# First halves of K's and Q's weights ahead of b1 in the transfer queue, their products in alternation, and all queues ordered anew from there

## The chip, the core and the metric

The kernel runs on one core of one Trainium2 chip. The core has a matrix engine (PE, or TensorE; its weight loads are shown apart as PEld), a vector engine (DVE, or VectorE), an activation engine (ACT, or ScalarE), a third elementwise engine (POOL, or GpSimd), and a queue engine (SP, or SyncE) that issues all transfers of this kernel. Each engine works through its own list of instructions in order, and waits at an instruction until the semaphores it needs have reached their counts. The metric is the time of the whole program on the device, in microseconds (us), smaller is better. Of several executions the median is given.

## The reference

Two transformer layers over 2048 rows of 512 columns, each with an attention and an MLP part, both layers with the same weights; all in bfloat16.

```python
def _A_ref(x, wqkv, wo):
    B, S, D = x.shape
    H = 32; Dh = D // H; W = 256
    qkv = (x @ wqkv).reshape(B, S, 3, H, Dh).transpose(2, 0, 3, 1, 4)
    q, k, v = qkv[0], qkv[1], qkv[2]
    scores = jnp.einsum("bhqd,bhkd->bhqk", q, k) * (Dh ** -0.5)
    idx = jnp.arange(S)
    mask = (idx[:, None] - idx[None, :] >= 0) & (idx[:, None] - idx[None, :] < W)
    p = _softmax(jnp.where(mask[None, None], scores, -1e9), axis=-1)
    o = jnp.einsum("bhqk,bhkd->bhqd", p, v)
    return o.transpose(0, 2, 1, 3).reshape(B, S, D) @ wo

def _B_ref(x, w1, b1, w2, b2):                 # F = 1792
    h = _gelu(jnp.einsum("bsd,df->bsf", x, w1) + b1)
    return jnp.einsum("bsf,fd->bsd", h, w2) + b2

x = A_x
x = x + _A_ref(_layernorm(x), A_wqkv, A_wo)
x = x + _B_ref(_layernorm(x), B_w1, B_b1, B_w2, B_b2)
x = x + _A_ref(_layernorm(x), A_wqkv, A_wo)
x = x + _B_ref(_layernorm(x), B_w1, B_b1, B_w2, B_b2)
```

Attention looks back over a window of 256 rows. There are 32 heads of 16 columns.

## The kernel before, in words

**Tiles and blocks.** The rows are cut into 16 tiles of 128; two layers make 32 tile steps (tau 0 to 31), and two tiles are a block (b 0 to 15; blocks 0 to 7 are the first layer). For each block the program contains, in this order of writing: layer norm (statistics on DVE, lines 591 and 593; the inverse root on ACT for the first two tiles and on POOL or DVE plus POOL afterwards, lines 596 to 609; the normalised tile `xn`, line 619), the transposed copy `xnTA` (for the first four tiles by PE and an evacuation, lines 631 and 580/582; for the others by a transposing transfer, line 624), the Q and K products (four groups of eight products of 256 columns, line 645) and V's (two groups of four products of 512 columns). Q and V are copied out of the accumulator by DVE (line 580) or ACT (line 582); K's evacuation on DVE (line 679) also spreads even and odd heads by `parmask`. V is copied a second time by a transfer, shifted by half a tile (`Vs`, line 694).

**Attention.** Per block ten groups of scores (five in blocks 0 and 8, line 746); each is exponentiated by ACT in two instructions of 128x1024 (line 753). Windows' edges are masked by a product with a 0/1 tile on DVE or POOL (line 774). Two output products per block (line 796) fill a pair of accumulator banks each; DVE transposes them out (line 805), takes the reciprocal of the sums (line 809), DVE or POOL normalises (line 813), DVE transposes back (line 819); the output projection and the residual (line 841) follow.

**MLP.** Ten jobs of two or four tiles. Of fourteen groups of the first product, six get their bias from DVE (line 863) and are passed through the GELU in pairs (line 866), eight go through ACT at once with bias and GELU (line 871). The bias `b1` comes as 14 rows of 128 (line 563), is transposed on PE (line 564) and copied to `b1T` by DVE (line 566). POOL adds `b2` to the residual (line 879), DVE adds the second product (line 886), and in the second layer the tile is stored (line 890). ACT loads a table whenever it goes from exponentials to GELUs or back.

**Transfers at the start.** All input and weight loads are issued by SP: X in pieces of one, one, two and then four tiles (line 540); the weights of Q, K in halves of 256 columns and those of V in one piece (line 545, 256 KB a half, 512 KB for V); Wo (line 559), W1 in three pieces (line 561), b1 (line 563), W2 in four pieces (line 570), b2 (line 573). Eighteen small products on a zeroed tile keep PE running until the first real one (line 531).

**What sets the order.** Nothing is issued in the order of writing. Each operation is a node (`_Plan.add`), numbered as it is written, 3097 in all. Three tables decide the rest: `_ORDER` is a permutation of all nodes, and each engine's queue is the part of it that belongs to that engine; `_ALT` lists the nodes that run on their second engine instead of their first; `_BANKS` deals the eight accumulator banks to the groups in the order in which they are allocated. The semaphores that each instruction waits for are derived from these tables and the operands.

```python
for i in _ALT:
    nodes[i]["eng"], nodes[i]["fn"] = nodes[i]["alts"][1]
banks = iter(_BANKS)
...
for i in _ORDER:
    nd = nodes[i]
    assert nd["deps"] <= seen
```

The second engine is ACT for an evacuation of Q, V or a transposed copy, POOL for a mask or a normalisation, and DVE for the addition before the inverse root; the first is DVE in the first four cases and POOL in the last.

## Time and profile before

| | |
|---|---|
| median of 3 runs | 442.81 us (441.93, 442.81, 443.56) |
| the profiled execution, its own time | 441.99 us |
| its span in the trace | 440.2 us |
| ACT's exponentials (line 753) | 284.0 us busy, 300 instructions |
| score products (line 746) and output products (line 796) | 1920 and 3840 |
| transfers over the span | 23.25 MB |

The profile is of one execution of the core. "Busy" is the time in which an engine has an instruction under way; a PE product has a tail in which the next already runs, so its mean duration is more than its cost. "Idle before" is the time an engine waited ahead of an instruction, with the instruction or transfer that released it, as far as the trace tells. The chain of waits goes back from the last instruction, at each step to what released it.

### The profile page before, as it was taken

To read this page: it belongs to the slowest core of one execution; us is meant where nothing else is said; L and a number is where in the kernel's file an instruction comes from. 1 tells how busy PE (TensorE), PEld (TensorE's weight loads), DVE (VectorE), ACT (ScalarE), POOL (GpSimd) and SP (SyncE) were. 2 spreads that over 40 slices of the span, in tenths; PEclk is the share of its full clock that TensorE was granted. 3 is DMA by queue.
4 is the path that set the end of the run, shared out by engine and by line. 5 is a ranking of instruction groups with operands and counts; after the bars stand their busy time and mean duration, and the time that the engine had idled before them with its cause. 6 is when DMAs were issued, how large, how long until landed. Compare 5 with 4: busy or idle time off the path is not lost.

```text
span 440.2 us, 16933 instructions
## 1 busy us (share of the span) xinstructions
PE 423.4 (96%) x7593; PEld 232.0 (53%) x7593; DVE 340.6 (77%) x638; ACT 386.1 (88%) x457; POOL 212.7 (48%) x236
## 2 busy tenths in 40 slices
PE   8998999988799998999999999999999999999997
PEld 4555657544444454554454455464555464444675
DVE  7998798888776599966798878867887576746762
ACT  4998999999989999889898989998897988999533
POOL 3466445363452584712566354724728165804411
DMA  7697422004101013021031021100321014003002
GB/s 232 189 179 219 87 63 45 20 10 74 35 3 38 3 34 68 17 46 25 3 70 26 1 58 25 42 14 11 67 39 20 20 39 105 14 1 85 12 0 73
DMA packets 48117, 23.25 MB, mean 53 GB/s; under 512 B 33197, under 2 KB 48045, under 8 KB 48045
## 3 DMA queue, kind: packets, MB, share of 16 engines
q1 hardware_dynamic: 48044, 22.17, 22.3%
q8 instruction: 60, 0.98, 0.9%
q14 instruction: 13, 0.10, 0.1%
HBM read 8.00 MB, written 2.10 MB: 23 GB/s over the span
## 4 chain that ended last, share of the span: by engine, by line
PE 86%; ACT 7%; DVE 3%; DMA 1%; issue 1%; SPq 1%; POOL 0%
PE ps L645 67%; PE ps L746 10%; PE ps L796 9%; ACT E L753 7%; DMA Wqkv_sb<-in_A_wqkv_dram 1%; DVE OD L805 1%; DVE E L774 0%; ACT QT L582 0%; DVE gT L863 0%; DVE stat L591 0%; DVE X L841 0%; SPq L540 0%; POOL Nb L813 0%; SPq L545 0%; DVE OT L819 0%
## 5 line engine op out<-in xcount | busy, mean ns | idle before, releaser
L753 ACT ACTIVATE E<-ps 128x1024 bf16<-128x1024 f32 x300 | 284.0, 1034 | 26.0 <-PE ps L746 25.1
L774 POOL TENSOR_TENSOR E<-E,mask 128x512 bf16<-128x512 bf16 (+2 forms) x111 | 120.9, 1106 | 89.5 <-ACT E L753 89.5
L645 PE MATMUL ps<-W_sb,gT 128*128 128x512 bf16 (+1 forms) x462 | 118.0, 374 | 0.2 <-DVE OD L805 0.2
L645 PE MATMUL ps<-xnTB,W_sb 128*128 128x512 bf16 (+1 forms) x560 | 111.7, 337 | 0.6 <-ACT E L753 0.5
L645 PEld LDWEIGHTS ps<-xnTB,W_sb 128*128 128x128 bf16 x560 | 51.7, 98 | 41.9 <-issue 2.7
L645 PE MATMUL ps<-xnTA,Wqkv_sb 128*128 128x256 bf16 x512 | 70.7, 273 | 0.5 <-DMA Wqkv_sb<-in_A_wqkv_dram 0.2
L774 DVE TENSOR_TENSOR E<-E,mask 128x512 bf16<-128x512 bf16 (+2 forms) x125 | 59.8, 498 | 13.4 <-ACT E L753 13.0
L746 PE MATMUL ps<-QT,KT 32*128 32x128 bf16 (+3 forms) x1920 | 60.0, 231 | 8.6 <-ACT E L753 5.2
L645 PEld LDWEIGHTS ps<-W_sb,gT 128*128 128x128 bf16 x462 | 41.1, 98 | 41.1 <-issue 3.9
L746 PEld LDWEIGHTS ps<-QT,KT 32*128 32x128 bf16 x1920 | 28.4, 92 | 58.5 <-ACT E L753 35.5
L645 PEld LDWEIGHTS ps<-xnTA,Wqkv_sb 128*128 128x128 bf16 x512 | 47.5, 98 | 20.4 <-issue 2.3
L805 DVE STREAM_TRANSPOSE OD<-ps 128x1024 f32<-128x1024 f32 x32 | 39.8, 1245 | 20.3 <-PE ps L796 19.7
L879 POOL TENSOR_TENSOR Xb<-X,b2all 128x512 f32<-128x512 bf16 x32 | 37.7, 1180 | 34.3 <-DVE X L886 33.9
L871 ACT ACTIVATE gT<-ps,b1T 128x512 bf16<-128x512 f32 (+1 forms) x80 | 42.6, 609 | 9.3 <-PE ps L645 9.2
L796 PE MATMUL ps<-E,Va 64*17 64x128 bf16 (+3 forms) x1920 | 43.3, 230 | 1.8 <-issue 0.8
L813 POOL TENSOR_TENSOR Nb<-OD,Rc 128x512 bf16<-128x512 f32 x25 | 26.4, 1057 | 38.1 <-DVE Rc L809 29.2
L796 PE MATMUL ps<-E,Vs 64*17 64x128 bf16 (+3 forms) x1920 | 44.0, 230 | 0.0
L591 DVE BATCH_NORM_STATS2 stat<-X 128x6 f32<-128x512 bf16 x64 | 42.9, 677 | 0.7 <-DMA X<-in_A_x_dram 0.3
L796 PEld LDWEIGHTS ps<-E,Va 64*17 64x17 bf16 x1920 | 36.8, 84 | 11.6 <-issue 9.0
L679 DVE TENSOR_TENSOR KT<-ps,parmask 128x1024 bf16<-128x1024 f32 x32 | 38.6, 1208 | 3.6 <-PE ps L645 3.6
L863 DVE TENSOR_SCALAR gT<-ps,b1T 128x512 bf16<-128x512 f32 (+1 forms) x60 | 36.7, 631 | 5.7 <-PE ps L645 5.3
L796 PEld LDWEIGHTS ps<-E,Vs 64*17 64x17 bf16 x1920 | 37.5, 84 | 0.1
(53 smaller groups left out, 353.4 us busy)
## 6 DMA issues: line engine op xcount, KB each, us to landing
Vs<-Va SPq DMA_DIRECT2D x64, 68.0 KB, 2.0
W_sb<-in_B_w_dram SPq DMA_DIRECT2D x4, 512.0 KB, 4.7
out_dram<-X SPq DMA_DIRECT2D x15, 128.0 KB, 1.9
X<-in_A_x_dram SPq DMA_DIRECT2D x3, 512.0 KB, 6.8
Wqkv_sb<-in_A_wqkv_dram SPq DMA_DIRECT2D x4, 256.0 KB, 5.0
W_sb<-in_B_w_dram SPq DMA_DIRECT2D x2, 384.0 KB, 7.1
W_sb<-in_B_w_dram SPq DMA_DIRECT2D x1, 768.0 KB, 5.7
Wqkv_sb<-in_A_wqkv_dram SPq DMA_DIRECT2D x1, 512.0 KB, 7.7
```

The costliest lines, as they stand in the source:

```text
L591: add("dve", lambda e, B, t=t, k6=k6: e.bn_stats(stat6[:, k6, :], X[:, t, :]), reads=["X%d" % t], writes=["st%d" % k6], key="bs%d" % (k + j))
L645: r = e.matmul(ps[:, B[g][0], cols], lhsT, rhs, start=st, stop=sp)
L679: add("dve", lambda e, B, g=g, i=i: e.tensor_tensor(out=KT[:, kb, 2 * i : 2 * i + 2].rearrange("p c m a q -> p a (c m) q"), in0=ps[:, B[g] ...
L746: x = e.matmul(ps[:, bk[r], o : o + n], KT[rows, kb, c, m].rearrange("p a q -> p (a q)"), QT[rows, c, q : q + n], start=True, stop=True)
L753: add("act", lambda e, B, g_=g_, gi=gi: e.activation(E[:, 2 * gi : 2 * gi + 2, e0 : e0 + 512], ps[:, B[g_][0] : B[g_][0] + 2, :], AF.Exp, ...
L774: fn = lambda e, B: e.tensor_tensor(out=Ew, in0=Ew, in1=Mw, op=ALU.mult)
L796: x = e.matmul(ps[32 * r : 32 * r + VW, B[g][par], c % 2 * 2 * P + lo : c % 2 * 2 * P + hi], V[rows, (2 * b + m // 2) % VR, c * HC + 2 * r ...
L805: add("dve", lambda e, B: e.transpose(OD[:, s].rearrange("p a c q -> p (a c q)"), ps[:, B[g][0] : B[g][0] + 2, :]), reads=["ps:" + g], wri ...
L813: return e.tensor_tensor(out=Nb[:, s, :].rearrange("p (k a d) -> p a k d", a=2, d=Dh), in0=sums[:, :, :, 0:Dh], in1=rc[:, :, :, None].to_b ...
L863: add("dve", lambda e, B, g=g, fc=fc: e.tensor_scalar(out=gT[:, fc, c0 : c0 + M], in0=ps[:, B[g][0], 0:M], scalar1=b1T[:, fc : fc + 1], sc ...
L871: add("act", lambda e, B, g=g, fc=fc: e.activation(gT[:, fc, c0 : c0 + M], ps[:, B[g][0], 0:M], AF.Gelu_apprx_tanh, bias=b1T[:, fc : fc + ...
L879: add("pool", lambda e, B, t=t, xs=xs: e.tensor_tensor(out=Xb[:, xs, :], in0=X[:, t, :], in1=b2all[:], op=ALU.add), reads=["X%d" % t, "b2a ...
```

## The change

Only the three tables differ. The nodes, and so all operations, sizes and operands, are the same. 2822 of the 3097 places of `_ORDER` hold another node, 59 entries of `_ALT` are exchanged for 59 others, and 407 of the 658 entries of `_BANKS` differ. The beginnings:

```diff
 _ORDER = [
-    15, 34, 5, 0, 6, 14, 35, 7, 33, 28, 38, 29, 47, 8, 18, 23, 9, 36, 3, 26, 31, 10, 57, 37, 11, 22, 1, 40, 4, 24, 2,
-    58, 59, 61, 17, 42, 62, 21, 60, 65, 41, 63, 19, 64, 68, 55, 32, 66, 107, 39, 69, 67, 20, 105, 50, 70, 48, 30, 27,
-    53, 25, 106, 108, 71, 109, 49, 72, 110, 73, 16, 74, 114, 81, 75, 82, 111, 83, 84, 115, 85, 86, 116, 112, 87, 88,
...
+    15, 34, 5, 8, 6, 0, 33, 35, 7, 18, 24, 9, 3, 16, 38, 10, 11, 29, 37, 12, 21, 4, 1, 36, 19, 2, 14, 57, 40, 22, 47,
+    28, 58, 59, 61, 25, 42, 31, 62, 60, 65, 53, 17, 63, 64, 30, 27, 68, 41, 26, 66, 105, 69, 39, 67, 23, 107, 20, 50,
+    32, 70, 106, 108, 109, 71, 55, 81, 110, 82, 72, 83, 13, 114, 84, 111, 73, 74, 85, 115, 75, 86, 87, 48, 112, 116,
...
 _ALT = [
-    67, 70, 75, 102, 109, 116, 121, 148, 165, 170, 185, 192, 198, 202, 211, 216, 337, 342, 370, 374, 378, 384, 389,
...
+    67, 70, 75, 102, 109, 116, 121, 148, 165, 192, 198, 202, 211, 216, 220, 327, 337, 342, 370, 374, 378, 379, 383,
...
 _BANKS = [
-    0, 1, 0, 1, 0, 2, 3, 2, 3, 5, 7, 0, 6, 5, 3, 2, 5, 4, 2, 4, 2, 3, 3, 5, 0, 1, 2, 6, 1, 5, 2, 4, 6, 1, 0, 2, 4, 6,
...
+    2, 5, 6, 5, 0, 5, 0, 3, 5, 3, 5, 3, 4, 0, 5, 4, 5, 0, 3, 0, 5, 7, 3, 0, 4, 1, 6, 2, 5, 4, 1, 4, 2, 6, 7, 4, 0, 2,
...
```

Read by engine, with nodes by name:

- **SP's queue, the start.** Before: X tiles 0, 1, 2-3 (nodes 34, 35, 38), b1 (47), Q's first half (36), K's first half (37), K's second half (40), X 4-7 (42), V (41), X 12-15 (55), Q's second half (39), X 8-11 (50), W2's third piece, rows 8 to 10, 384 KB (53). After: X 0, 1, 2-3, K's first half (37), Q's first half (36), K's second half (40), b1 (47), X 4-7 (42), W2's third piece (53), V (41), Q's second half (39), X 8-11 (50), X 12-15 (55).
- **PE's queue, the start.** Before: Q's four instructions of two products each (71 to 74, a warming product before the last), then K's (81 to 84), a transpose of the input (115), K's second half begun (86), the other transpose (112), its rest, the first scores (195); b1's transposition (48) stands ahead of Q. After: Q, K, K, Q, K, K, Q, Q (71, 81, 82, 72, 83, 84, 73, 74), the transpose (115), two instructions of K's second half (86, 87), b1's transposition (48), the other transpose (112), the first scores (195), the rest of K's second half, and then K's first group of the next block, then Q's, then V's first product (98).
- **Engines exchanged.** 44 masks go from DVE to POOL and 40 from POOL to DVE. Eight normalisations go from POOL to DVE (among them the second of block 3) and two from DVE to POOL. Two Q evacuations (blocks 2 and 9) and two of V (tiles 4 and 27) go from ACT to DVE; five of Q (blocks 4, 8, 12, 13, 14), one of V (tile 21) and one transposed copy (tile step 62 of the last layer norm) from DVE to ACT. Six additions before the inverse root go from POOL to DVE, seven from DVE to POOL.
- **The rest of the queues.** The same operations on each engine, with neighbours exchanged: a node keeps its rank on PE within 24 places (2.2 on average), on ACT within 9, on DVE within 20, on POOL within 14 and on SP within 16. In SP's queue several of the shifted copies of V (tiles 6, 8 to 11) stand later among the transposing transfers than before. In block 4, two statistics and a reciprocal that stood between the first output transpose and the last mask ahead of the second output product on DVE stand elsewhere, and one mask has come between. The last instructions are as before: the fourteen products of tile 14 (tile step 30), their addition, and the store.

352 rows, old and new, of tables (_ALT, _BANKS, _ORDER) are left out of this document.

## The prediction

> **What bounds the kernel now.** I read the page's sums first, then the chain of waits, then busy time by stretch, and last the timeline of the first 15 us.
>
> ```profile
> span 440.2 us, 16933 instructions
> PE 423.4 (96%) x7593; PEld 232.0 (53%) x7593; DVE 340.6 (77%) x638; ACT 386.1 (88%) x457; POOL 212.7 (48%) x236
> PE 86%; ACT 7%; DVE 3%; DMA 1%; issue 1%; SPq 1%; POOL 0%
> ```
>
> PE is busy for all but 440.2 - 423.4 = 16.8 us, and 86% of the chain that ended last is PE. No list of orders removes a product, so a new order can only fill PE's idle time. The stretches say where that lies.
>
> ```profile
> 14.40:30.00 15.60, 14.41 (x289) 9.04 (x287) 15.06 (x27) 15.44 (x19) 9.50 (x11) 1.00 0.86 163
> 20.00:40.00 20.00, 18.01 (x434) 11.68 (x430) 19.01 (x35) 17.82 (x23) 11.35 (x14) 1.00 0.86 191
> ...
> 130.00:436.00 306.00, 303.11 (x5269) 160.48 (x5268) 229.12 (x422) 269.40 (x314) 149.41 (x156) 1.00 0.15 32
> 90.00:130.00 40.00, 33.92 (x866) 18.47 (x850) 32.83 (x62) 36.83 (x42) 18.17 (x21) 1.00 0.18 33
> ```
>
> Columns: length, busy us of PE, PE's weight load, DVE, ACT, POOL, then granted clock (full everywhere), DMA share, GB/s. From 130 to 436 us PE lacks 306.0 - 303.1 = 2.9 us; from 90 to 130 it lacks 6.1 us, with ACT the fuller engine (36.83 of 40; idle 3.17), and from 20 to 40 us 2.0. So this is a PE-bound kernel with a head of 130 us in which ACT, and in 20 to 40 us DVE (19.01 of 20), hold PE up. What the change does there decides; later it can at best win 2.9 us.
>
> **The change, part by part.** First the head, which the title names.
>
> ```profile
> 2.18 0.50 SPq L563 DMA_DIRECT2D b1raw<-in_B_b_dram  x1
> 2.72 1.49 SPq L545 DMA_DIRECT2D Wqkv_sb<-in_A_wqkv_dram  x3
> 5.91 1.08 ACT L582 ACTIVATE xnTA<-ps 128x512 bf16<-128x512 bf16 x2 [0.94 <-PE ps L631]
> 6.62 0.09 PEld L564 LDWEIGHTS ps<-ident,b1raw 14*128 14x128 bf16 x1 [0.64 <-issue]
> 7.05 0.83 PE L645 MATMUL ps<-xnTA,Wqkv_sb 128*128 128x256 bf16 x6
> 7.93 1.26 PE L645 MATMUL ps<-xnTA,Wqkv_sb 128*128 128x256 bf16 x10
> 9.22 1.22 DVE L679 TENSOR_TENSOR KT<-ps,parmask 128x1024 bf16<-128x1024 f32 x1 [0.36 <-PE ps L645]
> 9.58 0.11 PEld L645 LDWEIGHTS ps<-xnTA,Wqkv_sb 128*128 128x128 bf16 x2 [0.35 <-DMA Wqkv_sb<-in_A_wqkv_dram]
> 10.06 1.28 ACT L753 ACT_TABLE_LOAD   x1
> 11.35 1.94 ACT L753 ACTIVATE E<-ps 128x1024 bf16<-128x1024 f32 x2
> 12.88 1.03 PE L645 MATMUL ps<-Wqkv_sb,xnTA 128*128 128x512 bf16 x4
> 13.94 0.60 ACT L582 ACTIVATE Va<-ps 128x512 bf16<-128x512 f32 x1 [0.16 <-PE ps L645]
> ```
>
> *First product.* Without b1's 0.50 us and its gap ahead of them, the three weight loads are issued 0.54 us earlier. But the first product (7.05) starts on the end of ACT's copy of the transposed input (5.91 + 1.08 = 6.99), not on weights. **0.**
>
> *Alternation.* Six pairs of products, 12 at some 0.11 us (ten take 1.26 us less a tail of 0.16), finish K's first bank at about 8.5 instead of 9.2, so DVE can evacuate it once its normalisations are done, about 8.9, some 0.35 us earlier. Q's bank is full only after all 16, about 9.0, and ACT's copy of it then delays the next transpose copy and the table load, which sets the first exponential: 9.0 + 0.6 + 0.6 + 1.28 = 11.5 against 11.35. The earlier scores wait for ACT. The 0.35 us wait for K's second half at 9.58 goes, and buys nothing at ACT. **0** (ACT +0.13, covered by the next term; alone it would cost 0.13).
>
> *b1's transposition* now stands on PE ahead of a transpose of the input, the scores, and everything behind. Before, PE's weight load for it sat 0.64 us on no recorded releaser, to 6.62; identity and bank being long ready, I read this as b1's arrival, 4.4 us after its issue. Issued at about 3.7 it lands at 8.1 by that row; if it lands only with the 512 KB load behind it, about 10.5. Hidden until 9.6 (DVE's K evacuation ends about 10.1, and only then copies that transpose out). So 0 to +0.9; nearer the first, **+0.1**.
>
> *V's weights* now have 384 KB of W2 ahead of them.
>
> ```profile
> Wqkv_sb<-in_A_wqkv_dram SPq DMA_DIRECT2D x1, 512.0 KB, 7.7
> ...
> 12.00:13.00 1.00, 1.00 (x11) 0.88 (x9) 1.00 (x4) 1.00 (x2) 0.26 (x2) 1.00 1.16 319
> ```
>
> Issued at 4.82, they landed at 4.82 + 7.7 = 12.5, just ahead of their first product at 12.88. At 319 GB/s the 384 KB are 1.2 us; less the 0.54 us gained in front, they land near 13.2. PE gets there about 12.7 (scores after K's evacuation at 10.1, the last pair of K's first block, then from 10.9 the next block's 16 products at 0.11), stalls 0.5, and all behind it in PE's queue with it; ACT's copy of V follows 1.0 us after arrival, 14.2 against 13.94. From 14.4 to 30 us ACT is busy 15.44 of 15.60, so it carries: **+0.3** (0 to +0.9, the latter if nothing is gained in front).
>
> *Load that changes engine.* Up to the 80.9 us point, where the second MLP job's GELUs end, ACT loses one Q and one V evacuation (tile block 2), and gets one Q (block 4).
>
> ```profile
> L582 ACT ACTIVATE QT<-ps 128x512 bf16<-128x512 f32 x13 | 8.0, 615 | 2.9 <-PE ps L645 2.9
> L580 DVE CAST QT<-ps 128x512 bf16<-128x512 f32 x19 | 13.0, 682 | 6.7 <-PE ps L645 6.5
> L813 DVE TENSOR_TENSOR Nb<-OD,Rc 128x512 bf16<-128x512 f32 x7 | 5.1, 735 | 0.2
> L813 POOL TENSOR_TENSOR Nb<-OD,Rc 128x512 bf16<-128x512 f32 x25 | 26.4, 1057 | 38.1 <-DVE Rc L809 29.2 <-DVE statmv L593 8.9
> ```
>
> ACT, at 0.615 for either kind: -0.615 - 0.615 + 0.615 = **-0.6** (0 if PE holds that stretch; -1.2 if only the first 47 us count). DVE takes both, 2 x 0.68 us, and gives masks to POOL; queue for queue it has 0.7 us more ahead of block 1's first output transpose. In 20 to 40 us it has 1.0 us idle, so most is covered: **+0.3** (0 to +1.5, its surplus at block 3's last K evacuation).
>
> *The hole at 100 to 127 us.* The chain in order of time:
>
> ```profile
> 104.45 1.26 DVE OD L805
> 105.71 0.02 issue
> 105.73 0.36 DVE Rc L809
> 106.09 0.07 issue
> 106.16 1.06 POOL Nb L813
> ...
> 122.72 0.75 DVE gT L863
> 123.47 0.47 DVE E L774
> 123.94 0.66 DVE gT L863
> 124.60 0.47 DVE E L774
> ```
>
> The normalisation on POOL in this chain goes to DVE: 0.735 for 1.06, **-0.3** (0 if PE finds other work). The second wait is a DVE queue of bias additions and masks ahead of the attention's second output product. Ahead of it now stand neither two statistics (0.68) nor a reciprocal (0.34), but one mask more (0.47): **-0.3** (0 to -0.55).
>
> *All else*: 2822 of 3097 places in the order, most by a few ranks (PE 2 on average, ACT 1.5, DVE 3), 44 masks to POOL and 40 back, 8 normalisations to DVE and 2 back, 407 of 658 bank choices, the shifted V copies later among SP's transposes. Counted by products queued ahead, no score group or MLP job stands over 4 us elsewhere on PE, and the latest shifted V copies keep some 3.5 us before their use, on durations of before. Each swap can win or open a wait; PE's slack from 130 us on is 2.9 us in all: **0** (-1.2 to +1.2). The end is unchanged: output tile 14's last 14 products, its addition, its store.
>
> Sum: 0 + 0.1 + 0.3 - 0.6 + 0.3 - 0.3 - 0.3 + 0 = -0.5. The profiled execution took 441.99 us, of which 440.2 span and 1.8 around it; 441.99 - 0.5 = 441.5. Its runs' median is 442.81, 0.82 above the profiled one, so I forecast a median of **442.3**. Ends of the terms: -1.2 - 0.3 - 0.55 - 1.2 = -3.3 and 0.9 + 0.9 + 1.5 + 1.2 = +4.5.
>
> **The rivals.** *DVE becomes the bound in the head.* One mechanism: evacuations and masks moved onto a DVE that is 95% full in 20 to 40 us make it late, and it never catches up, as ACT cannot run ahead without its K and Q tiles. By queue sums DVE has 2.8 us more ahead of block 4's first output transpose (about 117 us): 442.8 + 2.8 = 445.6. It decides from block 3's K evacuations, near 40 us. Against it: 1.36 of the 2.8 are statistics that only moved forward, and from 90 to 130 DVE has 7.2 us idle. For it:
>
> ```profile
> L774 DVE TENSOR_TENSOR E<-E,mask x125: 229/426/1400, 20.3 to 410.2; 128x512 bf16<-128x512 bf16 x59, 128x768 bf16<-128x768 bf16 x47, 128x256 bf16<-128x256 bf16 x19
> L813 DVE TENSOR_TENSOR Nb<-OD,Rc x7: 681/693/1000, 30.5 to 390.6; 128x512 bf16<-128x512 f32 x7
> ```
>
> A mask on DVE takes 426 ns, but up to 1400, and a normalisation up to 1000; eight more of these at 0.3 us over median would add 2.4 us of DVE. The Trainium skill (SBUF — State Buffer, Who interferes with whom) gives a reason: a DVE instruction with two SBUF inputs contends with a GpSimd instruction that reads SBUF, and the later one blocks for the whole of it. The trace agrees in that the longest DVE mask is longer by 0.97 us than the median one; by that rule the step I price at -0.3 could be a loss of its own.
>
> *New waits in the full part.* If PE loses twice the 2.9 us from 130 to 436, the time is 445.7; for it, banks and order were all dealt anew; against it, queues there stand nearly as before.
>
> *The hole closes.* If the shorter chains of 100 to 127 us let ACT run through, its 3.17 us idle in 90 to 130 go: 442.8 - 3.2 = 439.6. Against it: ACT's waits in that window are six for scores, the longest 0.9 us, more than the two chains.
>
> ```profile
> ACT E L753 <- PE ps L746: 3.1, 6, 0.9
> ```
>
> *It doesn't do what it says.* The first product waits for ACT, the first exponential for the table; all else cancels: 442.8.
>
> **How the numbers follow.** Forecast 0.40, nothing moves 0.13, both within 0.5% of 442.81 (440.6 to 445.0, about what a measurement here can tell from no change): same 0.53. The hole closes 0.20: faster. DVE late 0.17 and new waits 0.10: slower 0.27. The likeliest alone lies in 440.6 to 444.6. The range reaches to the faster rival and a little over the slower two: 439.6 to 446.2; some 0.15 is left outside.
>
> **What would show it.** First product still near 7.05 and first exponential 11.3 to 11.6; V's first product waiting for a load, ACT's copy of V near 14.2; b1's load on PE before 9.6 without a wait; the second job's GELUs ending near 80.5; PE busy over 34.3 in 90 to 130, with the transpose, reciprocal, normalisation, transpose chain 0.3 us shorter. I am wrong if PE's idle time from 130 to 436 differs from 2.9 by over 1.2 us, or DVE goes full in 20 to 50 us and block 1's first output transpose starts over 1 us after 38.0.

## The result and the profile after

The changed kernel took 443.62 us (median of 15 runs, 442.72 to 444.33), the kernel before on the same chip 442.43 (15 runs, 441.84 to 444.40). The ratio is 1.0021, 95% interval 1.0012 to 1.0031: 0.9 us slower (0.5 to 1.4; the two medians lie 1.2 apart), where the sum said 0.5 us faster. The same two programs run again (e5 and e6 below) gave 442.40 and 443.58 us. Among their executions at full granted clock (some of before's lack it for a few us, see the last section) the medians are 442.31 and 443.59 us, 1.3 us apart.

From the page of the changed kernel: span, busy time, and the shares of the chain that ended last.

```profile
span 441.0 us, 16846 instructions
PE 415.9 (94%) x7526; PEld 232.0 (53%) x7593; DVE 342.4 (78%) x636; ACT 388.4 (88%) x460; POOL 212.5 (48%) x235
PE 75%; ACT 14%; DVE 7%; issue 2%; DMA 0%; POOL 0%; DVEq 0%
```

PE's 415.9 us is not a gain: 67 of its 7593 products are missing in this trace (x7526), while all 7593 weight loads are there. The profiled execution was also the fastest of the 15 (442.72 us). So I read the busy time by stretch from the second profile of the changed kernel (e6), which has every product. Columns as in the prediction.

```profile
14.40:30.00 15.60, 13.80 (x281) 8.71 (x280) 14.95 (x26) 14.38 (x18) 10.57 (x10) 1.00 0.75 180
20.00:40.00 20.00, 18.41 (x436) 11.70 (x434) 18.92 (x37) 17.57 (x21) 13.17 (x14) 1.00 0.75 188
90.00:130.00 40.00, 34.38 (x871) 18.32 (x870) 35.12 (x66) 37.53 (x42) 15.30 (x19) 1.00 0.17 30
130.00:436.00 306.00, 303.27 (x5266) 160.48 (x5265) 230.65 (x418) 272.90 (x319) 152.24 (x158) 1.00 0.15 33
```

From 14.4 to 30 us ACT is busy 14.38 instead of 15.44, and PE 13.80 instead of 14.41: there the head lost time. From 130 us on PE lacks 306.0 - 303.27 = 2.73 us, as good as the 2.9 before, so by busy time nothing happened there. That is misleading, as e11 shows. From 90 to 130 us PE is busy 34.38 instead of 33.92, which the forecast had put at over 34.3.

The timeline of the changed kernel's first profile, with the lines that answer to those of before, and the chain at 105 us.

```profile
5.49 1.27 ACT L582 ACTIVATE xnTA<-ps 128x512 bf16<-128x512 bf16 x2 [0.46 <-PE ps L631]
6.93 1.91 PE L645 MATMUL ps<-xnTA,Wqkv_sb 128*128 128x256 bf16 x16 [0.36 <-DMA Wqkv_sb<-in_A_wqkv_dram]
8.88 0.60 ACT L582 ACTIVATE QT<-ps 128x512 bf16<-128x512 f32 x1 [2.12 <-PE ps L645]
9.44 0.09 PEld L564 LDWEIGHTS ps<-ident,b1raw 14*128 14x128 bf16 x1 [0.21 <-issue]
9.98 1.28 ACT L753 ACT_TABLE_LOAD   x1
11.27 1.94 ACT L753 ACTIVATE E<-ps 128x1024 bf16<-128x1024 f32 x2
13.71 0.60 ACT L582 ACTIVATE Va<-ps 128x512 bf16<-128x512 f32 x1
15.98 1.58 DVE L619 TENSOR_SCALAR xn<-X,statmv,rstd 128x512 bf16<-128x512 bf16 x2
16.22 1.18 POOL L774 TENSOR_TENSOR E<-E,mask 128x512 bf16<-128x512 bf16 x1 [0.36 <-ACT E L753]
16.30 1.25 DVE L619 TENSOR_SCALAR xn<-X,statmv,rstd 128x512 bf16<-128x512 bf16 x1
17.48 0.68 DVE L580 CAST QT<-ps 128x512 bf16<-128x512 f32 x1
18.21 0.41 PE L746 MATMUL ps<-QT,KT 32*128 32x128 bf16 x24 [0.69 <-DVE QT L580]
...
105.07 1.25 DVE L805 STREAM_TRANSPOSE OD<-ps 128x1024 f32<-128x1024 f32 x1 [0.57 <-PE ps L796]
106.36 0.35 DVE L809 RECIPROCAL Rc<-OD 128x32 f32<-128x32 f32 x1
106.75 0.69 DVE L813 TENSOR_TENSOR Nb<-OD,Rc 128x512 bf16<-128x512 f32 x1
107.47 0.71 DVE L819 STREAM_TRANSPOSE OT<-Nb 128x512 bf16<-128x512 bf16 x1
```

Three things are to be seen. The first product is now released by a transfer. At 16 us two normalisations on DVE take 1.58 us, the second of them 1.25, while POOL's mask runs from 16.22 to 17.40; the copy of Q queued behind them ends at 18.16, and PE waits 0.69 us for it. And from the first output transpose to the transpose back the chain takes 107.47 - 105.07 = 2.40 us, against 107.25 - 104.45 = 2.80 before, where the transpose back waits for POOL; that step came as forecast. Its end in before:

```profile
107.25 0.71 DVE L819 STREAM_TRANSPOSE OT<-Nb 128x512 bf16<-128x512 bf16 x1 [1.17 <-POOL Nb L813]
```

**How the traces are compared.** For each score and output group I took the start of its first weight load on PE, less the work queued ahead of it (0.109 us a product of 256 columns, 0.2165 of 512, 0.33 a score group, 0.887 or 1.387 an output group), and the difference between two traces. This is called PE's lag: how much more idle time PE has had up to that group. The start varies between executions of one program, so in the table the end of ACT's first two copies of the transposed input (5.49 + 1.27 = 6.76 above) is the zero point, and e5 the reference.

| PE's lag, us | 17.6 us | 55 us | 140 us | end |
|---|---|---|---|---|
| before, first profile | +0.09 | -0.38 | -0.35 | -0.28 |
| before, second (e5) | 0 | 0 | 0 | 0 |
| after, first profile | +0.81 | +0.28 | +0.17 | +0.73 |
| after, second (e6) | +1.62 | +1.06 | +0.74 | +1.45 |
| e4, mask waits | +0.15 | -0.32 | -0.44 | +0.01 |
| e8, loads repaired | +0.97 | +0.42 | +0.35 | +1.09 |
| e9, both | +0.07 | +0.03 | +0.04 | +0.57 |
| e18, alternation alone | +0.19 | +1.29 | +1.42 | +1.52 |
| e10, middle alone | -0.02 | -0.12 | +0.23 | +0.36 |
| e11, late part alone | 0.00 | -0.01 | -0.04 | +0.77 |
| e12, one normalisation | -0.08 | +0.12 | +0.08 | +0.46 |
| e16, 161 to 220 us | -0.08 | +0.06 | +0.17 | +0.17 |

Read so, all eight profiles whose head keeps before's order lie within 0.09 us of e5 at 17.6 us, and what chance does later is of the size of the first two rows, some 0.4 us. Left out of the table are profiles that hold something of their own, told below: a joint or a bank that holds PE up (e1, e2, e3, e13, e14 and e17, at the end +2.69, +2.15, +1.22, +0.37, +0.96 and +2.38), the clock (e15, +2.51; also e1 and e17), and one stall (e7, +1.44).

### The profile page after: what moved, and what is told of

The parts are those of the page before. It is cut to its first block, busy times and chain, and to the rows that moved or that the text cites. A ratio compares the mean times of both kernels' runs of the same rounds, so it can differ in the third digit from the quotient of the medians.

```text
span 441.0 us, 16846 instructions
## 1 busy us (share of the span) xinstructions
PE 415.9 (94%) x7526; PEld 232.0 (53%) x7593; DVE 342.4 (78%) x636; ACT 388.4 (88%) x460; POOL 212.5 (48%) x235
## 4 chain that ended last, share of the span: by engine, by line
PE 75%; ACT 14%; DVE 7%; issue 2%; DMA 0%; POOL 0%; DVEq 0%
PE ps L645 58%; ACT E L753 13%; PE ps L746 9%; PE ps L796 9%; DVE stat L591 2%; DVE KT L679 1%; DVE E L774 1%; DVE xn L619 1%; DVE gT L863 1%; DVE OD L805 1%; DVE X L841 1%; DMA X<-in_A_x_dram 0%; DVE X L886 0%; ACT QT L582 0%; DVE statmv L593 0%
## 5 line engine op out<-in xcount | busy, mean ns | idle before, releaser
L774 POOL TENSOR_TENSOR E<-E,mask 128x512 bf16<-128x512 bf16 (+2 forms) x115 | 125.9, 1106 | 97.9 <-ACT E L753 97.8
L645 PE MATMUL ps<-W_sb,gT 128*128 128x512 bf16 (+1 forms) x436 | 110.6, 373 | 2.6 <-issue 1.9
L645 PE MATMUL ps<-xnTB,W_sb 128*128 128x512 bf16 (+1 forms) x543 | 107.7, 335 | 2.8 <-issue 1.7
L645 PE MATMUL ps<-xnTA,Wqkv_sb 128*128 128x256 bf16 x512 | 69.8, 273 | 1.4 <-ACT E L753 0.5
L774 DVE TENSOR_TENSOR E<-E,mask 128x512 bf16<-128x512 bf16 (+2 forms) x121 | 58.6, 508 | 9.9 <-ACT E L753 9.4
L871 ACT ACTIVATE gT<-ps,b1T 128x512 bf16<-128x512 f32 (+1 forms) x80 | 43.5, 609 | 7.7 <-PE ps L645 7.5
L863 DVE TENSOR_SCALAR gT<-ps,b1T 128x512 bf16<-128x512 f32 (+1 forms) x60 | 37.1, 632 | 12.4 <-PE ps L645 10.8
L886 DVE TENSOR_TENSOR X<-Xb,ps 128x512 bf16<-128x512 f32 (+1 forms) x33 | 21.9, 665 | 24.8 <-PE ps L645 24.5
L813 POOL TENSOR_TENSOR Nb<-OD,Rc 128x512 bf16<-128x512 f32 x19 | 20.4, 1073 | 42.3 <-DVE Rc L809 34.0
```

What stands on the lines that cost most here:

```text
L645: r = e.matmul(ps[:, B[g][0], cols], lhsT, rhs, start=st, stop=sp)
L774: fn = lambda e, B: e.tensor_tensor(out=Ew, in0=Ew, in1=Mw, op=ALU.mult)
L863: add("dve", lambda e, B, g=g, fc=fc: e.tensor_scalar(out=gT[:, fc, c0 : c0 + M], in0=ps[:, B[g][0], 0:M], scalar1=b1T[:, fc : fc + 1], sc ...
L871: add("act", lambda e, B, g=g, fc=fc: e.activation(gT[:, fc, c0 : c0 + M], ps[:, B[g][0], 0:M], AF.Gelu_apprx_tanh, bias=b1T[:, fc : fc + ...
L886: add("dve", lambda e, B, gy=gy, t=t, xs=xs, lo=lo, hi=hi: e.tensor_tensor(out=X[:, t, lo:hi], in0=Xb[:, xs, lo:hi], in1=ps[:, B[gy][0], 0 ...
```

## The experiments

Only tables differ between the kernels, so most edits join the two orders: the first n nodes of one list, in the other's order and with its engines, then the rest. All times are medians in us beside before's on the same chip.

| | time | before | ratio, 95% interval |
|---|---|---|---|
| e1 head of after alone | 443.60 | 442.44 | 1.0024 [1.0012, 1.0036] |
| e2 after to 161 us | 443.69 | 442.44 | 1.0033 [1.0020, 1.0046] |
| e3 after from 161 us | 443.72 | 442.44 | 1.0029 [1.0018, 1.0040] |
| e4 after, mask waits | 443.21 | 442.44 | 1.0019 [1.0006, 1.0032] |
| e5 before again | 442.40 | 442.47 | 0.9999 [0.9986, 1.0012] |
| e6 after again | 443.58 | 442.47 | 1.0025 [1.0013, 1.0037] |
| e7 before to 18 us, then after | 442.67 | 442.47 | 0.9998 [0.9987, 1.0010] |
| e8 after, loads repaired | 443.33 | 442.47 | 1.0022 [1.0009, 1.0035] |
| e9 after, both repairs | 442.91 | 442.39 | 1.0013 [1.0004, 1.0021] |
| e10 after from 18 to 161 us alone | 442.61 | 442.39 | 1.0005 [0.9994, 1.0016] |
| e11 after from 161 us alone | 443.01 | 442.39 | 1.0011 [1.0002, 1.0020] |
| e12 before, one normalisation on DVE | 442.36 | 442.39 | 1.0006 [0.9987, 1.0024] |
| e13 before, the named change alone | 443.66 | 442.61 | 1.0026 [1.0014, 1.0038] |
| e14 the same, Q's weights first | 443.32 | 442.61 | 1.0022 [1.0010, 1.0034] |
| e15 after to 161 us, banks renamed | 444.18 | 442.61 | 1.0038 [1.0024, 1.0052] |
| e16 after from 161 to 220 us alone | 442.53 | 442.61 | 0.9999 [0.9988, 1.0011] |
| e17 before, b1 behind the loads | 443.31 | 442.29 | 1.0026 [1.0013, 1.0039] |
| e18 before, alternation alone | 443.19 | 442.29 | 1.0021 [1.0012, 1.0030] |

**e1 to e3: which part of the order?** `_ORDER` joined after 105 nodes (e1, about 12 us) and after 1149 (e2 and e3, about 161 us).

> The changed kernel's order for the first 105 nodes only (loads of K's and Q's halves ahead of b1, the alternation, b1's transposition behind K's second half, W2's third piece ahead of V's weights), the order of before from there. Theory (the title's change is good at the head, the loss comes behind it): first scores near 10.1 us, first exponential 11.3, V's first copy by ACT near 13.7 instead of 13.94, PE at the second score group of block 0 (17.5 before) 0 to 0.3 us earlier than before, end -0.3 to +0.2 us. Rival (the head itself costs: W2's piece delays what DVE needs): PE 0.4 us or more later at 17.5 us, end +0.4 or more.

> The changed kernel's three tables for the first 1149 nodes (up to some 161 us; at that point both orders have issued the same set of nodes), those of before from there. The first half of the change alone. Theory (some 0.3 us is lost up to 161 us as balance of a loss of 0.7 at 17 us and a gain of 0.5 near 105 to 120, and some 0.5 behind 260 us): span about +0.3 us over before, ratio 1.0005 to 1.0010. Rival one (all of the loss arises early): +0.9 us, ratio 1.002. Rival two (all of it late): 0, ratio 1.000.

> The tables of before for the first 1149 nodes, those of the changed kernel from there: the second half of the change alone. Theory: +0.5 us over before, ratio 1.0010 to 1.0015, PE's lag behind before rising by steps of about 0.1 us between 260 and 375 us. Rival one (all of the loss early): 0. Rival two (all of it late): +0.9, ratio 1.002.

As they stand, the time of e1 is its rival's, and those of e2 and e3 lie above every expectation. Each part alone cost as much as the whole, so the parts do not add up, and one reason is a flaw of e2 and e3. The row of e3 behind the joint, and the same group in e11, where the joint was made better:

```profile
163.07 0.41 PE L746 MATMUL ps<-QT,KT 32*128 32x128 bf16 x24 [0.72 <-ACT E L753]
```

```profile
162.34 0.41 PE L746 MATMUL ps<-QT,KT 32*128 32x128 bf16 x24
```

At the joint the score groups met banks that the other order had in use: 0.72 us in e3, and as much in e2, which neither kernel has. The program's time also stands further above its span in the five kernels that are joined at 161 us (e2, e3, e10, e11 and e15: 1.9 to 2.0 us by the median, against 1.7 to 1.8 in all others); why is open. Less both, e2 leaves some 0.3 us and e3 some 0.4. e1 is not free of its joint either: V's first weight load comes there at 13.89 us, behind exponentials that ended at 13.78, where the product ahead had started at 13.09: some 0.7 us that neither kernel has. So its lag of 1.43 us at 17.6 us is not the head's alone, and the head is better read from e7 to e9.

**e4: the mask on POOL.** Block 1's first mask waits for block 1's first two normalisations:

```diff
-            S_.op(nd["eng"], lambda e, fn=nd["fn"]: fn(e, B), reads=phys(nd["reads"]), writes=phys(nd["writes"]), dma=nd["dma"])
+            S_.op(nd["eng"], lambda e, fn=nd["fn"]: fn(e, B), reads=phys(nd["reads"]) + (["xn0", "xn1"] if nd["key"] == "mk1_0_0" else []), writes=phys(nd["writes"]), dma=nd["dma"])
```

> The changed kernel with one more wait: POOL's first mask of block 1 starts only when DVE has written the normalised tiles 4 and 5. Theory (that mask holds up the second of the two normalisations on DVE, 1.25 us instead of 0.41, and all of the jump of 0.7 us at the second scores of block 0 stands on it): the pair of normalisations takes 0.8 us instead of 1.58, PE is 0.6 to 0.8 us earlier than in the changed kernel at 17.5 us; at the end 0.3 to 0.7 us faster than the changed kernel, ratio to before near 1.001. Rival (the normalisation is long for another reason): still 1.2 us, nothing moves. Rival two (the jump is made good by 130 us anyway, where ACT paces): earlier by 0.7 at 17.5 us, end as the changed kernel, ratio 1.002.

```profile
16.34 0.74 DVE L619 TENSOR_SCALAR xn<-X,statmv,rstd 128x512 bf16<-128x512 bf16 x2
17.22 1.16 POOL L774 TENSOR_TENSOR E<-E,mask 128x512 bf16<-128x512 bf16 x1 [0.99 <-DVE xn L619]
18.02 0.41 PE L746 MATMUL ps<-QT,KT 32*128 32x128 bf16 x24
```

The pair takes 0.74 us again, the mask pays 0.99 us of waiting that nobody misses, and PE no longer waits for the copy of Q. The lag at 17.6 us falls from 0.81 and 1.62 to 0.15. The time falls by less than its interval. That POOL's mask is what makes the normalisation long is shown beyond this one place. In all twenty traces a normalisation of this line takes 0.37 to 0.42 us when POOL is idle beside it; 91 of 1280 take over 0.6 us, and each of the 91 begins while POOL has a mask or the addition of `b2` under way and ends 0.15 us after it.

**e5 and e6: the same two programs again.**

> The kernel before, unchanged, to see how far two profiles of the same program differ. If the head is the same in every execution, its PE stands within 0.1 us of the first profile at every score group. If the landing of the weights varies (in the experiments so far before's own head gave a first exponential at 11.35 and at 11.06 us, the third weight load landing at 9.54 and 8.40), PE differs by 0.3 to 0.7 us from about 10 us on, and part of the difference between the two kernels' first profiles is chance. Median ratio to the kernel before within 0.1% of 1.

> The changed kernel, unchanged, to see whether its first profile was typical. Theory (the first product waits for two weight loads instead of for the input's copy): first product 7.3 to 7.5 as in the three other profiles that have this order of transfers (7.50, 7.36, 7.28), first exponential 11.6 to 11.9, V's first product held 0.3 to 0.8 us by its load. Rival (the first profile is typical and the head costs nothing before the normalisation pair at 16 us): first product 6.9 to 7.0, first exponential 11.2 to 11.3. Time as before, 443.6 in either case.

The second profile of the changed kernel, and then of before:

```profile
5.71 1.08 ACT L582 ACTIVATE xnTA<-ps 128x512 bf16<-128x512 bf16 x2 [0.73 <-PE ps L631]
7.80 1.91 PE L645 MATMUL ps<-xnTA,Wqkv_sb 128*128 128x256 bf16 x16 [1.27 <-DMA Wqkv_sb<-in_A_wqkv_dram]
9.74 0.60 ACT L582 ACTIVATE QT<-ps 128x512 bf16<-128x512 f32 x1 [2.94 <-PE ps L645]
12.14 1.94 ACT L753 ACTIVATE E<-ps 128x1024 bf16<-128x1024 f32 x2
14.56 0.60 ACT L582 ACTIVATE Va<-ps 128x512 bf16<-128x512 f32 x1
```

```profile
6.10 1.08 ACT L582 ACTIVATE xnTA<-ps 128x512 bf16<-128x512 bf16 x2 [1.09 <-PE ps L631]
7.24 0.91 PE L645 MATMUL ps<-xnTA,Wqkv_sb 128*128 128x256 bf16 x6
8.62 0.60 ACT L582 ACTIVATE QT<-ps 128x512 bf16<-128x512 f32 x1 [1.44 <-PE ps L645]
10.33 1.28 ACT L753 ACT_TABLE_LOAD   x1
11.63 1.94 ACT L753 ACTIVATE E<-ps 128x1024 bf16<-128x1024 f32 x2
43.31 1.03 PE L645 MATMUL ps<-xnTB,W_sb 128*128 128x256 bf16 x8 [0.55 <-DMA xnTB<-xn]
```

In the second execution of the changed kernel the input's copies ended at 5.71 + 1.08 = 6.79, as in the first, but the first product started at 7.80, released by the weights. The reason is in the new queue: K's weights are issued first, and Q's product comes first, so it needs the second load. How much that costs differs from execution to execution. In the seven profiles with this order of loads (both of after, e1, e2, e4, e13, e15) the product started 0.05 to 0.17 us behind the copies in four, and 0.37, 0.84 and 1.01 us behind in e15, e1 and e6, each time 0.14 us behind the landing of the second load. In the eight with before's head it started 0.05 to 0.22 us behind the copies (7.18, 7.24 here). So the expectation's 7.3 to 7.5 missed, and two of the three profiles that it was drawn from (e2, e4) had late copies, not late weights.

The wait at 43.31 for a transposing transfer of before's second profile is not in its first (0.17 us at 42.92, and not for a transfer): this is the 0.4 us of chance. The trace tells of the landing in sixteen parts. In before's first profile all had landed at 41.73, 2.5 us after the issue; in e5 fifteen at 41.70 and the last at 43.22.

**e7 and e8: head undone, and loads repaired.** e7 has before's order for the first 162 nodes (to 18 us). e8 moves two transfers of after: Q's first weights (node 36) ahead of K's (37), W2's piece (53) behind X's last pieces.

```diff
-    15, 34, 5, 8, 6, 0, 33, 35, 7, 18, 24, 9, 3, 16, 38, 10, 11, 29, 37, 12, 21, 4, 1, 36, 19, 2, 14, 57, 40, 22, 47,
-    28, 58, 59, 61, 25, 42, 31, 62, 60, 65, 53, 17, 63, 64, 30, 27, 68, 41, 26, 66, 105, 69, 39, 67, 23, 107, 20, 50,
+    15, 34, 5, 8, 6, 0, 33, 35, 7, 18, 24, 9, 3, 16, 38, 10, 11, 29, 36, 37, 12, 21, 4, 1, 19, 2, 14, 57, 40, 22, 47,
+    28, 58, 59, 61, 25, 42, 31, 62, 60, 65, 17, 63, 64, 30, 27, 68, 41, 26, 66, 105, 69, 39, 67, 23, 107, 20, 50, 32,
```

> The order of before for the first 162 pieces of work (to about 18 us: order of transfers, products in turn, all queues), that of after from there on. Theory (the head's new order costs 0.5 to 1 us, the rest gains about 0.5 by block 3's normalisation on DVE): 442.0 to 442.6, faster than after by about 1 us and no slower than before. Rival (the cost lies in the full part from 160 us on, where after's queues alone gave 443.7): 443.4 to 443.8, as after. A third reading, that any seam between two orders costs some 0.7 us by itself, would also give 443.4 or more; it is told from the rival by PE's lag, which then rises at 18 us instead of past 160.

> After, with two transfers moved: Q's first weights ahead of K's (the first product uses Q's), and the 384 KB of W2 behind all of X and V's weights. Theory (late weights cost the head): first product at 7.0 as soon as the input's copy is there, V's first product without a wait, PE's lag against before about 0.5 us less than after's from 15 us on, 443.0 to 443.3. Rival (DVE and not the weights sets the head): first product earlier, the lag at 20 us unchanged, 443.5 to 443.7.

e7 is no slower than before by its interval (up to 0.4 us), 0.9 us from e6 (443.58 - 442.67): the head holds most of the loss. It does not hold all: at full clock e7's median lies 0.4 us over before's, and from 140 us to the end its lag rises by 0.8 us as in the kernels with the late order below. Its profile ran long by one stall in the middle of an output product (e2 has a like one of 1.20 us at 30.15), so its lag is left out of the table:

```profile
29.26 0.26 PE L796 MATMUL ps<-E,Vs 64*17 64x192 bf16 x4 [1.38 <-issue]
```

In e8 the first product again follows the input's copies at once (0.06 us), and the lag at 17.6 us is still 0.97, against 0.81 and 1.62 in the two profiles of after: the mask and the alternation are left.

**e9: both repairs.** e8's order and e4's wait.

> After, with both repairs of the head together: Q's first weights ahead of K's and the piece of W2 behind all of X and V's weights, and POOL's mask of block 1's first score group waiting until block 1's first two normalisations are done. Theory (after's head costs 0.35 us by late weights and 0.7 us by the normalisation pair of 1.58 us instead of 0.73): 442.4 to 442.8, no longer slower than before, PE's lag on before at 20 us within 0.3 us of nothing, the pair at 0.73 to 0.80. Rival (each repair gains alone but the next wait takes its place): 443.1 to 443.3, as the better of the two alone.

442.91 lies between the two expectations. Against e6 the repairs brought 0.67 us back (443.58 to 442.91), more than each alone. At full clock, beside before's of the same chip, after is 1.3 us slower, e4 0.7, e8 1.0 and e9 0.5: the mask's wait brings some 0.5 us, the loads some 0.3, and both together 0.7, so the two add up as far as medians of some ten runs tell. The trace has the theory's pair (0.73 us) and lag (0.07 at 17.6 us), and says where the rest is: 0.04 at 140 us, 0.57 at the end. What is left is late.

**e10, e11 and e16: the stretches behind the head.** For these and e15 the banks behind each joint were renamed, so that a group gets the bank that was freed longest ago.

> The order of after only from 18 to 161 us, that of before ahead of and behind it; the PSUM banks behind each seam are renamed so that each score group again gets the bank that came free longest ago. Theory (the middle gains 0.2 to 0.4 us, by block 3's normalisation on DVE and the shorter queue behind it; head and late part carry the whole loss): 441.9 to 442.3, faster than before by 0.2 to 0.5; PE's lag -0.2 to -0.4 at 130 us and unchanged from there on. Rival (the middle gains nothing that lasts): 442.4 to 442.6.

> The order of before until 161 us and that of after from there, as in e3, but with the banks behind the seam renamed. In e3 the first score group behind the seam waited 0.72 us for an exponential that held its bank. Theory (after's order loses 0.4 to 0.6 us between 240 and 375 us by stalls of 0.1 to 0.2 us): 442.8 to 443.1, no step of PE's lag at 164 us, +0.4 to +0.6 from 240 to 375 us. Rival (late part free, e3's 443.7 was the seam alone): 442.4 to 442.6.

> The order of after only from 161 to 220 us, the one stretch in which its PE gained on before (0.1 to 0.3 us by every profile of it), before's ahead and behind. Theory (the gain is the order's own): PE's lag falls by 0.1 to 0.3 us between 161 and 240 us and stays, 442.2 to 442.4, which a time cannot tell from before. Rival (the gain is borrowed from later work): the lag comes back by 260 us, 442.4 to 442.7.

The middle alone gains nothing (lag +0.23 at 140 us, before's two profiles -0.35 and 0). The late part costs 0.5 us by time (0.1 to 0.9; 0.4 by the medians of the spans) and 0.8 by the trace, all of it behind 235 us. It belongs to the order: in all eight profiles with after's order from 161 us to the end the lag rises by 0.76 to 1.04 us between 261 and 387 us, in the eleven others beside e5 by 0.02 to 0.23. In e16, the stretch before that, PE gains 0.2 us until 235 us and loses as much from 310 us on, where before's order rules again; its time is before's. Two of the places where e11 loses, by PE's weight loads:

```profile
266.16 0.23 PEld L746 LDWEIGHTS ps<-QT,KT 32*128 32x128 bf16 x12 [0.54 <-ACT E L753]
315.19 0.12 PEld L796 LDWEIGHTS ps<-E,Va 64*17 64x17 bf16 x4 [0.58 <-DMA Vs<-Va]
```

The same places in before:

```profile
266.41 0.20 PEld L746 LDWEIGHTS ps<-QT,KT 32*128 32x128 bf16 x12 [0.42 <-DVE X L886]
314.97 0.09 PEld L796 LDWEIGHTS ps<-E,Va 64*17 64x17 bf16 x4 [0.42 <-issue]
```

0.42 us is what the weight load stands behind the product ahead of it in the ordinary case; what is above it is a stall (0.58 - 0.42 = 0.16, and the load itself is longer by 0.03). The product ahead is on the books as running meanwhile, so PE's busy time shows none of it. The one at 315.19 waits for a shifted copy of V.

**e12: the step that I was surest of.** Node 738, block 3's second normalisation, is taken off `_ALT` of before and so runs on DVE.

> Before, with one instruction changed: block 3's second normalisation of the attention's output on DVE instead of POOL, as in after. Theory (my -0.3, in the chain that holds PE at 105 us): PE's lag -0.3 to -0.4 from 108 us on, 442.1. Rival 1 (ACT or the next wait sets PE there): lag back to nothing by 125 us, 442.4 to 442.5. Rival 2 (DVE held up by POOL through the shared port makes it dearer): the normalisation over 1.0 us, 442.6 or more.

```profile
104.70 1.25 DVE L805 STREAM_TRANSPOSE OD<-ps 128x1024 f32<-128x1024 f32 x1 [0.41 <-PE ps L796]
106.37 0.69 DVE L813 TENSOR_TENSOR Nb<-OD,Rc 128x512 bf16<-128x512 f32 x1
107.09 0.71 DVE L819 STREAM_TRANSPOSE OT<-Nb 128x512 bf16<-128x512 bf16 x1
```

The chain is 2.39 us long instead of 2.80, and by 116 us PE stands where it stood ahead of it (lag 0.12 at 101 us, 0.08 at 140). Rival 1 is right: the next wait took over. Rival 2 is out, at 0.69 us for the normalisation.

**e13, e14, e17, e18: the two parts that the change is named for.** In before's order: loads K, Q, K ahead of b1, alternation, b1's transposition later (e13); the same with Q's load first (e14); the loads and b1's transposition without alternation, Q first (e17); alternation alone (e18):

```diff
-    53, 25, 106, 108, 71, 109, 49, 72, 110, 73, 16, 74, 114, 81, 75, 82, 111, 83, 84, 115, 85, 86, 116, 112, 87, 88,
+    53, 25, 106, 108, 71, 109, 49, 81, 110, 82, 16, 72, 114, 83, 84, 111, 73, 74, 115, 75, 85, 86, 116, 112, 87, 88,
```

> Before, with nothing changed but what the change is named for: K's and then Q's first weights and K's second ones ahead of b1 in the transfer queue, the eight products of Q and K in after's alternation, b1's transposition behind them. W2's piece, the engines' loads, banks and everything from the first scores on stay as before. Theory (the first product needs the second load, and Q's copy on ACT, ahead of the copy that the table load waits for, comes after all eight pairs): first product 7.2 to 7.6 instead of 6.8 to 7.2, first exponential 11.5 to 11.9 instead of 11.1 to 11.6, 442.7 to 443.0. Rival (my prediction's: the input's copy sets the first product, alternation costs ACT 0.13 at most): first product 6.8 to 7.1, 442.4 to 442.6.

> The same with Q's first weights ahead of K's. Theory (of the two causes only the alternation is left): first product 6.8 to 7.2 as before, Q's copy on ACT still after all 16 products, 8.8 to 9.1 instead of 8.1 to 8.6, first exponential 11.3 to 11.6, 442.5 to 442.8. Rival (the loads were the whole of it): first exponential 11.1 to 11.3, 442.4.

> Before, with b1's load behind the three weight loads (Q's, K's, K's) and its transposition behind on PE, products in turn as before. Theory (the input's copy sets the first product, so earlier weights buy nothing and cost nothing): from the end of ACT's copies of the transposed input to the first exponential 4.35 to 4.45 us as in before (e13 4.76, e14 4.83), 442.3 to 442.6. Rival (the move of b1 is part of the loss: its transposition comes ahead of one of the input's and makes it late): 4.6 or more, 442.9 or more.

> Before, with the eight pairs of products of Q and K in after's alternation and nothing else; transfers as before. Theory (Q's copy on ACT comes after 16 products instead of 8, and ahead of the copy for which the table load waits): from the end of ACT's copies of the transposed input to Q's copy 2.0 to 2.4 us instead of 1.35 to 1.44, to the first exponential 4.7 to 4.9 instead of 4.35 to 4.45, 443.0 to 443.6 as in e13 and e14. Rival (it needs both): 4.5 or less, 442.4 to 442.7.

All four are 0.7 to 1.1 us slower than before, but the times of e13, e14 and e17 are not what they were meant to measure. In e13:

```profile
10.51 0.16 PE L564 MATMUL ps<-ident,b1raw 14*128 14x14 bf16 x1 [0.61 <-ACT xnTA L582]
```

b1's transposition kept the bank that it has in before, and at its later place ACT's third copy of the transposed input frees that bank: PE stood 0.61 us there in e13 and e14, 0.56 in e17. In the changed kernel it has another bank and waits for nothing (9.44 above). So they show that moving b1 is dear with the wrong bank, not that it is dear; the transfers alone remain unmeasured. The times of e13 and e14 lie above both of their expectations, and e17's is its rival's, by the wait just told. In e17 Q's copy started 1.35 us after the end of the input's copies, and 1.35 to 1.51 us in the eight profiles with before's head, so earlier weights bought nothing. In e13, with K's load first, the first product followed the copies by 0.05 us, so the late weights that its theory put there did not come in this execution. e18 moves neither b1 nor a load; one entry of `_BANKS` differs, and V's first weight load comes behind an exponential at 12.96, some 0.2 us later than the product ahead of it (12.62) allowed:

```profile
6.10 1.09 ACT L582 ACTIVATE xnTA<-ps 128x512 bf16<-128x512 bf16 x2 [1.12 <-PE ps L631]
9.42 0.60 ACT L582 ACTIVATE QT<-ps 128x512 bf16<-128x512 f32 x1 [2.24 <-PE ps L645]
10.52 1.28 ACT L753 ACT_TABLE_LOAD   x1
11.82 1.94 ACT L753 ACTIVATE E<-ps 128x1024 bf16<-128x1024 f32 x2
44.04 1.03 PE L645 MATMUL ps<-xnTB,W_sb 128*128 128x256 bf16 x8 [1.10 <-ACT E L753]
```

From the end of the input's copies (7.19) to Q's copy it takes 2.23 us instead of 1.44 in e5, to the table load 3.33 instead of 3.15 in e5 and 3.07 in before's first profile, to the first exponential 4.63 instead of 4.36 to 4.45: the alternation costs about 0.2 us at the first exponential, less than the theory's 4.7 and more than the rival's 4.5. e18's time is 0.9 us over before (0.5 to 1.3), and the head explains 0.19 of it (17.6 us). The rest of this profile's lag is the 1.10 us of waiting at 44 us, the place of e5's 0.55. The row puts it down to an exponential, but what ended it was the same transposing transfer as in e5: fifteen parts had landed at 41.89 us and the last at 43.95, 4.6 us after the issue, and the product started 0.09 us later, as it did 0.09 us after the landing in e5 (43.22, 43.31). This profile is 0.7 us slower than e18's median, so it does not say what the median holds; that stays open.

**e15: after to 161 us again.**

> The order of after until 161 us, before's from there, as e2 but with the banks behind the seam renamed. Theory (three separate losses: head about 0.9 us at 18 us, of which the stretch to 125 us gives some 0.3 back; late part 0.5 to 0.8): 442.9 to 443.2, no 0.72 us wait at 164 us, PE's lag constant from 130 us to the end. Rival (the late loss is not the late order's own but follows from the head's lateness): PE's lag rises between 240 and 375 us here too, 443.5.

444.18 misses both expectations, but the question is answered by the trace: from 177 us to the end the lag rises by 0.3 us, of which 0.2 by 188 us, against 0.6 and 0.7 in after's two profiles. So most of the late loss belongs to the late order. Why this kernel is slower than the whole change stays open beyond the 0.2 us outside its span; its profile holds something else, told in the last section.

No mixture beat before. e10, e12 and e16, made of the stretches that looked like gains, lie within 0.1% of it.

## Why the prediction was wrong

The range held the time, but it was 6.6 us wide, and the direction was wrong: 0.5 us faster was forecast, 0.9 slower came. The step that failed is the head. The prediction let ACT's smaller load carry everything there (-0.6), started the first product on the input's copy whatever the loads did (0), and had no term for one DVE instruction that meets POOL's. In its place the runs show PE 0.81 and 1.62 us late at 17.6 us, 0.7 to 0.9 of it by one pair of normalisations (e4, e9) and up to 1.0 us by late weights in some executions. By time the two repairs bring 0.7 us back. The second step is the hole (-0.6), which gave no time, the third the late order, put at 0, which costs some 0.5 us.

- **"First product. 0."** Wrong in kind. I wrote that the first product starts on the end of ACT's copy of the transposed input, not on weights. That was read from before, where the first product uses the first load. In the new order it uses the second. It started 0.17 us after the copies in the first profile (6.76 to 6.93), 1.0 us in the second (6.79 to 7.80). The diff showed it: K's load first, Q's product first.
- **"Alternation. 0 (ACT +0.13, covered)."** Right mechanism, and nearly the size: about +0.2 at the first exponential (e18). The cover was wrong; it was to be ACT's smaller load.
- **"b1's transposition, +0.1."** Right that it waits for nothing: on PE at 9.44, with 0.21 us of issue ahead of its weight load. The arrival was misread. In before b1 had landed at 4.66 us, and the transposition at 6.62 waited for ACT's first copy, which ended at 6.50 and, as later in e13, freed its bank; before's own row says so:

```profile
6.65 0.16 PE L564 MATMUL ps<-ident,b1raw 14*128 14x14 bf16 x1 [0.34 <-ACT xnTA L582]
```

That b1 then landed at 8.01 and 8.64 us in the changed kernel, near the forecast 8.1, is luck.

- **"V's weights, +0.3."** Not shown in the changed kernel. ACT's copy of V came at 13.71 and 14.56, on both sides of the predicted 14.2, but in neither profile did a product of V wait for a load: V's weights landed at 12.50 and 12.82, and the second copy is late because all of the head is. The load itself does come later, at 12.4 to 13.2 us in the six profiles with W2's piece in front against 11.3 to 11.9 in seven of the eight with before's head. In the eighth, before's first, it landed at 12.53, and that one the forecast started from. The wait came in e4 (V's weights at 13.22, 0.33 us).
- **"Load that changes engine: ACT -0.6, DVE +0.3."** The -0.6 did not come. The second job's last GELU ended at 81.48 and 82.20 us instead of 80.89 and 81.46; I had said 80.5. ACT did less, but was fed late. Of the sign of DVE's term I was right and of its place wrong: not the length of DVE's queue held PE, but a single pair of normalisations, 1.58 us instead of 0.73, at 16 us. It costs 0.7 to 0.9 us by then (after's first profile against e4, 0.81 to 0.15; e8 against e9, 0.97 to 0.07). This term was missing altogether. The prediction named the rule that explains it for another instruction. The Trainium skill (SBUF — State Buffer, Who interferes with whom) says that a DVE operation of this kind, too, can take the port it shares with GpSimd, and that whichever of the two comes later then waits for the whole of the other. The traces agree: the second normalisation began 0.08 us behind POOL's mask, took 1.25 us instead of 0.41 and ended 0.15 us after the mask, in every profile with this overlap, and e4 takes it away. They differ in one thing: a wait for the whole mask would leave 0.4 us of work behind it, and the trace shows 0.15, with POOL's ends only roughly known. Before's own trace had the sign, in this line of its times by instruction that I did not read (least, median and longest ns):

```profile
L619 DVE TENSOR_SCALAR xn<-X,statmv,rstd x63: 316/406/1257, 5.2 to 421.9; 128x512 bf16<-128x512 bf16 x63
```

- **"The hole at 100 to 127 us, -0.3 and -0.3."** The normalisation's chain was 0.40 us shorter, as forecast, and from 101 to 140 us the lag falls by 0.49 and 0.69 us in the two profiles of after. It falls by 0.2 to 0.6 in five of the other six with after's order there and full clock, and not at all in e10. But in all eight it had risen by 0.14 to 0.38 us between 55 and 101 us, so that over the whole stretch from 55 to 140 us the order gains between -0.35 and +0.33 us, on both sides of nothing. In e12, where the normalisation alone moves, the fall is 0.04. So the shorter chain by itself gave no time; which of the other exchanges give and take in this stretch is not separated.
- **"All else: 0."** Its late part is +0.5 by time (e11), within the +-1.2 that I gave, and consists of stalls of 0.1 to 0.2 us.

By the trace the two profiles of after are 0.81 and 1.62 us late at 17.6 us, get 0.5 and 0.6 back by 55 us and 0.1 and 0.3 by 140, and lose 0.6 and 0.7 from there on: 0.73 and 1.45 at the end, against 0.9 and 1.1 by the two ratios (1.0021 and 1.0025 of 442.4). The rival "DVE becomes the bound in the head" was the nearest in place (DVE in front of PE at 18 us, block 1's first output transpose at 39.10 instead of 38.04), but it priced a queue's sum, 2.8 us. "New waits in the full part" had the late mechanism, at 2.9 us instead of 0.5. Of my own signs two spoke against me, this transpose and the GELUs, though DVE was not full: 18.92 of 20 us from 20 to 40 us, 19.01 before. PE's idle time from 130 us on (2.73 us) did not, and could not, as busy time hides such stalls.

## What to carry to other kernels

Ask of the first instruction of a reordered start which load it needs, not which it needed before, and take a second profile before trusting a start that hangs on transfers. Where DVE and POOL work side by side, look at each instruction's longest time beside its median, and treat a DVE normalisation that begins during a POOL mask as lasting until the mask ends. A shorter chain is worth only what the next wait leaves of it: find that wait before pricing the chain.

## What the hardware showed that I had not expected

- The same transfers land at different times from run to run. Between the two profiles of after, the second weight load landed at 6.80 and 7.66 us; the end of the input's two copies lay between 6.62 and 7.24 us over all profiles. Of the transposing transfer that the first MLP products wait for, at 43 to 44 us, the last of sixteen parts landed 1.5 to 2.1 us behind the others in ten of twenty profiles.
- In three profiles of twenty PE's granted clock was half of full for one stretch of 3.4 us: from 108.2 us in e15, 108.5 in e17 and 117.2 in e1. In e15, where the stretch lies across both windows (0.82 and 0.84 are the means over 5 us each):

```profile
105.00:110.00 5.00, 3.47 (x53) 1.34 (x38) 3.42 (x5) 3.91 (x6) 3.09 (x3) 0.82 0.65 89
110.00:115.00 5.00, 4.83 (x61) 2.06 (x59) 3.85 (x10) 3.73 (x5) 1.99 (x3) 0.84 0.18 28
```

The lag grew by 1.1 to 1.5 us between 101 and 140 us in these three, and stayed. A mean clock of 0.996 over the program, which is what 3.4 us at half clock make of 440, was recorded in 23 of 143 other executions of before and in none of the changed kernel's 27. It happened in the stretch where PE is idle in many pieces, none longer than 1.3 us, and seventeen profiles with the same pieces have a full clock there; what sets it off stays open. The Trainium skill (TensorE: Matmul & The Clock Gate, Part 1) lets the clock fall after an idle window of about 3.4 us; no stretch here is idle that long, so by that rule it should have stayed. The same part also tells of a kernel whose clock went back and forth because PE was idle for short times between products; it gives no measure by which the runs here could be told apart.
